# An attention and bilinear-FFN kernel whose instruction order is written by a planner: another transfer model in the planner, earlier start of the first pairs, and fewer dependencies on the first FFN products

## The chip, the cores and the metric

The kernel runs on one core of a Trainium2 chip. The metric is the device time of one execution in microseconds, here the median of three timed runs. Beside the timed runs there is one profiled execution, and everything that is read from a trace belongs to that one execution.

TensorE is called PE, its weight loads PEld, VectorE DVE, ScalarE ACT, GpSimd POOL and SyncE SP. Each engine runs its own list of instructions strictly in order, so an instruction that waits holds back all that stand behind it in the same list. SP and ACT also issue the transfers (DMAs); an issue row stands under SPq or ACTq.

## The reference

Inputs are q, k, v of shape (8, 12, 448, 64), two gains of 64 numbers, and three FFN weights in double precision: `w_a` and `w_b` (768 x 1536) and `w_out` (1536 x 768).

```python
q_n = q / sqrt(mean(q*q, -1) + 1e-6) * g_q          # the same for k with g_k
scores = q_n @ k_n.T / sqrt(64)
attn = softmax(scores)                              # over the keys
x = (attn @ v)  -> rows of (batch*seq, heads*64) = (3584, 768)
out = ((x @ w_a) * (x @ w_b)) @ w_out               # (3584, 768), float32
```

## The kernel before, in words

**Pairs of heads.** The 96 heads are worked off as 48 pairs, p = 0 to 47, six pairs to a batch row. For a pair, SP loads q, k and v (224 KB each, two buffers of each kind). `normalize(p)` squares q and k on ACT (`sq`, L435), sums the squares on DVE (`ms`, L442), takes the mean (L449), raises it to the power -0.5 on POOL (L453), and multiplies q by it on DVE (`qn`, L457). The k side is not multiplied: its factor goes into the exponential as a scale. `transposes(p)` turns k and qn on PE (`pt`, L486); ACT copies both to `qkT` (L491, L493). `scores` are four chunks of keys per pair on PE (`sc`, L506), each followed by two exponentials on ACT (`ET`, L512). `values` multiplies them with v (`o`, L527). For the first twelve pairs the sums over the keys are made on PE with a matrix of ones (`su`, L562); later pairs add on DVE and POOL first.

On PE a pair p makes two chains that are not interrupted: chain A holds the scores of chunks 0 and 1 of pair p and the values and sums of chunks 2 and 3 of pair p-1; chain B holds the scores of chunks 2 and 3 of pair p and the values and sums of its chunks 0 and 1. The transposes of the next pair stand between chains.

**The division.** The key sums of a pair are copied out of PSUM by ACT (`rec`, L581), spread over partitions by a transfer (`few`, L587), inverted on DVE (L598), written to DRAM (`inv`, L591) and read back to all partitions (L595). Then DVE multiplies the outputs with them (`x`, L624). I call these three transfers the round trip of the reciprocals.

**Weights.** `factors(n)` makes one of 18 sets of weights (12 of `w_a` and `w_b`, n = 0 to 11, and 6 of `w_out`, n = 12 to 17) from doubles: two loads of 768 KB issued by ACT, one ACT step (L268), six DVE steps (L269 to L277) and four DVE additions (L377), and a store of the finished set (`kept`, 1344 KB) issued by ACT. The words land in room that later tiles use: `hraw` in the tile of `hT` for the "early" sets, `lraw` in the tile `late` for the others. There are three `st` buffers for finished sets. The FFN works on two batch rows at once (four times, beta = 0 to 3), each matrix product made of seven products of half size (`pq`, L779, then `po`, L707); T2, T3 and T4 are differences of the four quarters of x, made by DVE in `combine` (L643).

**What sets the order.** No engine list is written by hand. Every piece of work is entered with `op(engine, us, key, emit, reads, writes, ...)`, and `Plan.run` (L70) is a list scheduler: it keeps a clock per engine, takes the engine whose next piece can start first, and among the pieces that can start about then the one with the lowest key. Its costs are the numbers `us`; a transfer of `kb` kilobytes is costed on a line of its own per issuing engine (L143 to L147). The planned times are used for the order alone; on the chip each instruction waits for what it depends on. `GATES` and `seq` (L877) say behind which pair's scores each weight set may be loaded and in which order; `WARM` says how many groups of four 128x128 matmuls (`warm`, L868) are put on PE with the lowest urgency.

Of the kernel before, what the change touches and what calls it, by code (L numbers as in the profile page):

```python
# [9 lines left out]
FP32 = mybir.dt.float32  # L10
# [15 lines left out]
class Plan:  # L26
# [10 lines left out]
    LANES = 8  # L37
    LAG = 0.1
# [31 lines left out]
    def run(self):  # L70
# [18 lines left out]
        opened, free, modes, cands, dma, port = {}, {}, {}, {}, {"SP": 0.0, "ACT": 0.0}, 0.0  # L89
# [21 lines left out]
        while any(cands.values()):  # L111
# [56 lines left out]
def kernel(  # L168
# [127 lines left out]
    def fast_body(ld, wk, ps_s, ps_o, ps_mm, dram):  # L296
# [4 lines left out]
        WARM = 12  # L301
# [40 lines left out]
        def factors(n, key, early, after):  # L342
# [16 lines left out]
            for part in range(2):  # L359
# [9 lines left out]
                op("ACT", 0.45, key - 2.5, load, after, [f"{row}/{part}"], kb=768)  # L369
# [38 lines left out]
        def loads(p, nm):  # L408
# [12 lines left out]
            op("SP", 0.5 if nm != "k" else 0.9, p - (1.8 if nm == "v" else 2.0), emit, [], [t], new=[t], kb=230)  # L421

        def normalize(p):

            ms, key = tile_of(f"ms{p}", "ms", 3), p - NORM
            for s, nm in enumerate("qk"):
                sq = tile_of(f"sq{nm}{p}", "sq", 1)

                def square(nm=nm):
# [4 lines left out]
                    if p < LEAD or SQUARE == "ACT":  # L434
                        nc.scalar.activation(t, flat, AF.Square)  # L435
                    else:
                        two[SQUARE].tensor_tensor(t, flat, flat, ALU.mult)

                def reduce(nm=nm, s=s):
                    if s == 0:  # L440
                        rs[p] = wk.tile([SP, 2, 2 * NJ], FP32, tag="ms", name="ms", bufs=3)
                    nc.vector.tensor_reduce(rs[p][:, s], xs["sq", nm, p], AX, ALU.add)  # L442
                e = "ACT" if p < LEAD else SQUARE
                op(e, {"ACT": 0.65, "POOL": 1.05, "DVE": 0.7}[e], key, square, [f"{nm}{p}"], [sq], new=[sq], lock=e != "ACT")
                op("DVE", 0.69, key, reduce, [sq], [ms], new=[ms] if s == 0 else [])

            def mean():
                msf = rs[p].rearrange("p s n -> p (s n)")
                nc.vector.tensor_scalar(msf, msf, 1.0 / D, 1e-6, ALU.mult, ALU.add)  # L449

            def root():
                msf = rs[p].rearrange("p s n -> p (s n)")
                nc.gpsimd.tensor_tensor(msf, msf, expo, ALU.pow)  # L453
# [8 lines left out]
            op("DVE", 0.18, key, mean, [], [ms])  # L462
            op("POOL", 2.95, key, root, [], [ms])
            qn = tile_of(f"qn{p}", "qn", 1)
            op("DVE", 0.7, key, apply, [ms, f"q{p}"], [qn], new=[qn], lock=True)
# [33 lines left out]
        def scores(p, c, chain):  # L499
# [16 lines left out]
            op("ACT", 1.12, p, exps, [sc, f"ms{p}"], [E], new=[E])  # L516
# [30 lines left out]

        def sums_over_keys(p, cs, chain):
# [19 lines left out]
            if p % (2 * HP) == 2 * HP - 1:  # L568
# [28 lines left out]
            op("SP", 0.8, p - 3.0, spread_out, [t], [few], new=[few], kb=20, dmas=2)  # L597
            op("DVE", 0.25, p - 3.0, lambda: nc.vector.reciprocal(fews[0], fews[0]), [], [few])  # L598
            op("SP", 0.4, p - 3.0, leave, [few], [f"inv{p}"], kb=20)
            op("SP", 0.8, p - 3.0, come_back, [f"inv{p}"], [t], kb=230, dmas=2)  # L600
# [8 lines left out]
        def put_out(p):  # L609
# [16 lines left out]
            op("DVE", 0.65, p, divide, [f"su{p}" if p % (2 * HP) == 2 * HP - 1 else f"rec{p}"], [f"{x}/{c}"], lock=True)  # L626
# [136 lines left out]
        def quarter_products(beta, key, m, ab, st, at, names, h):  # L763
# [6 lines left out]
            def product(bank, f, x, start, stop):  # L770
# [11 lines left out]
                op("PE", KH * S / 595, key, emit, [f"{st}/{(0, 0, 0, 0, 4, 5, 6)[f]}", *parts(x), *parts(T3), *parts(T4)], [nm, "ffn"], new=[nm] if start else [], mode="full")  # L782
# [94 lines left out]
        GATES = [0, 0, 1, 2, 3, 5, 7, 9, 10] + [12] * 9  # L877
        seq = [12, 13, 14, 15, 16, 0, 1, 2, 3, 4, 5, 6, 7, 17, 8, 9, 10, 11]
        for p in range(NP + 1):
            for x, n in enumerate(seq):  # L880
                if p == GATES[x]:
                    factors(n, x * 1.1 + 0.5, x < 8, [f"scored{p - 1}"] if p else [])
            if p < NP:
                for nm in "qkv":
                    loads(p, nm)
            if p == 0:
# [166 lines left out]
```

## Time and profile before

| what | value |
|---|---|
| median of three timed runs | 1647.89 us (1640.82 to 1650.4) |
| profiled execution, its own time | 1654.08 us |
| its span (first to last instruction) | 1652.2 us |
| mean granted PE clock | 0.989 of full |
| PE busy | 1604.7 us, 97% of the span |
| DVE / ACT / POOL busy | 729.3 / 432.7 / 401.8 us |
| moved by transfers | 191.21 MB |

PE's busy time includes matmuls that run at a lower clock; a matmul group of the same form at two durations tells of it. The idle time of an engine is listed with what ended it. Start times in a timeline are microseconds from the span's start. The profiled execution lies 6.2 us above the median of the timed runs.

### The profile page before, as it was taken

What the parts mean: (1) busy time and instruction counts of PE and PEld (TensorE: products, weight loads), DVE (VectorE), ACT (ScalarE), POOL (GpSimd) and SP (SyncE); (2) the same over time, 40 slices, a digit from 0 to 9 for tenths busy, and PEclk for the clock granted to TensorE, in tenths of its full rate; (3) what the DMA queues carried; (4) which work ended last, traced back from release to release, by engine and by line L of the source; (5) the groups of instructions that cost most, each with busy time, mean ns of one, the idle gap of its engine ahead of it and who ended that gap; (6) DMA issues with size and microseconds to landing.
All of it is one profiled execution on the core that took longest, in us unless ns stands there. A gap on an engine that the chain in (4) does not pass through costs nothing.

```text
span 1652.2 us, 15068 instructions
## 1 busy us (share of the span) xinstructions
PE 1604.7 (97%) x5546; PEld 786.7 (48%) x5546; DVE 729.3 (44%) x992; ACT 432.7 (26%) x777; POOL 401.8 (24%) x200
## 2 busy tenths in 40 slices
PE   7888799999999999999999999999999999999998
PEld 5333344455444455555444455555544555555554
DVE  4776657789567532222267541122235422222331
ACT  4666563311355610000255620000034000000000
POOL 3232354211366620100265630000133000100000
PEclk9999999999999999999999999999999999999999
DMA  5676325354433443212232333322222332222121
GB/s 183 229 228 219 122 68 183 100 209 149 147 97 99 117 141 123 100 67 100 80 97 85 107 104 129 109 71 96 96 68 81 110 134 100 96 71 91 70 103 50
DMA packets 131656, 191.21 MB, mean 116 GB/s; under 512 B 62196, under 2 KB 120308, under 8 KB 121844
## 3 DMA queue, kind: packets, MB, share of 16 engines
q1 hardware_dynamic: 103828, 137.06, 25.8%
q10 hardware_dynamic: 27744, 53.09, 8.9%
q8 instruction: 46, 0.75, 0.2%
q14 instruction: 38, 0.31, 0.1%
HBM read 154.01 MB, written 35.94 MB: 115 GB/s over the span
## 4 chain that ended last, share of the span: by engine, by line
PE 83%; DMA 7%; DVE 6%; issue 1%; ACT 1%; POOL 1%; SPq 1%; ACTq 0%; DVEq 0%; POOLq 0%
PE pq L779 43%; PE po L707 23%; PE sc L506 6%; PE o L527 6%; DMA inv<-few 2%; PE su L562 2%; DMA few<-rec 2%; PE pt L486 2%; DMA rec<-inv 1%; DVE x L643 1%; DMA k_sb<-in_k_dram 1%; DVE st L377 1%; POOL ms L453 1%; DVE st L277 1%; DVE su L572 1%
## 5 line engine op out<-in xcount | busy, mean ns | idle before, releaser
L779 PE MATMUL pq<-x,st 128*128 128x448 f32 x2016 | 768.3, 542 | 3.2 <-DVE t L836 3.2
L779 PEld LDWEIGHTS pq<-x,st 128*128 128x128 f32 x2016 | 381.9, 191 | 378.7 <-issue 368.3
L512 ACT ACTIVATE ET<-sc,ms 112x448 f32<-112x448 f32 x384 | 216.2, 637 | 128.4 <-PE sc L506 117.5
L707 PE MATMUL po<-st,hT 128*128 128x384 f32 x744 | 247.3, 488 | 0.0
L542 POOL TENSOR_TENSOR sum<-sum,ET 112x896 f32<-112x896 f32 x72 | 162.2, 2253 | 197.9 <-DVE sum L540 180.1
L453 POOL TENSOR_TENSOR ms<-ms,expo 112x16 f32<-112x16 f32 x48 | 152.6, 3180 | 214.7 <-DVE ms L449 203.5
L506 PE MATMUL sc<-qkT 64*112 64x448 f32 x768 | 175.1, 573 | 26.2 <-ACT ET L512 14.1
L827 POOL TENSOR_TENSOR hT<-hT,t 128x448 f32<-128x448 f32 x24 | 27.9, 1164 | 676.4 <-DVE t L825 676.4
L707 PEld LDWEIGHTS po<-st,hT 128*128 128x128 f32 x744 | 139.4, 190 | 102.2 <-issue 9.5
L527 PE MATMUL o<-ET,v_sb 112*64 112x448 f32 x768 | 168.1, 560 | 1.0 <-ACT x L620 1.0
L707 PE MATMUL po<-st,fin 128*128 128x384 f32 x432 | 145.1, 489 | 0.0
L801 ACT COPY hT<-pq 128x448 f32<-128x448 f32 x24 | 12.8, 532 | 447.0 <-PE pq L779 447.0
L506 PEld LDWEIGHTS sc<-qkT 64*112 64x112 f32 x768 | 61.2, 175 | 120.0 <-issue 79.0
L707 PEld LDWEIGHTS po<-st,fin 128*128 128x128 f32 x432 | 80.6, 190 | 59.3 <-issue 7.0
L527 PEld LDWEIGHTS o<-ET,v_sb 112*64 112x64 f32 x768 | 51.1, 140 | 106.9 <-issue 101.5
L442 DVE TENSOR_REDUCE ms<-sq 112x8 f32<-112x512 f32 x96 | 65.1, 678 | 73.5 <-ACT sq L435 69.7
L727 DVE TENSOR_TENSOR o_sb<-fin,po 128x384 f32<-128x384 f32 x56 | 31.0, 554 | 149.9 <-PE po L707 146.2
L457 DVE TENSOR_TENSOR qn<-q_sb,ms 112x512 f32<-112x512 f32 x48 | 62.6, 1304 | 22.2 <-POOL ms L453 11.2
L839 POOL TENSOR_TENSOR hT<-hT,t 128x448 f32<-128x448 f32 x48 | 58.9, 1229 | 46.7 <-DVE t L836 46.7
L804 ACT COPY t<-pq 128x448 f32<-128x448 f32 x24 | 12.8, 533 | 187.2 <-PE pq L779 187.2
L832 DVE TENSOR_TENSOR hT<-U,pq 128x448 f32<-128x448 f32 x48 | 29.8, 621 | 68.2 <-PE pq L779 68.2
L836 DVE TENSOR_TENSOR t<-U,pq 128x448 f32<-128x448 f32 x48 | 29.6, 620 | 65.0 <-PE pq L779 63.9
(70 smaller groups left out, 980.8 us busy)
## 6 DMA issues: line engine op xcount, KB each, us to landing
st<-kept SPq DMA_DIRECT2D x36, 1344.0 KB
st<-kept_o SPq DMA_DIRECT2D x28, 1152.0 KB
kept<-st ACTq DMA_DIRECT2D x12, 1344.0 KB
q_sb<-in_q_dram SPq DMA_DIRECT2D x48, 224.0 KB
k_sb<-in_k_dram SPq DMA_DIRECT2D x48, 224.0 KB
v_sb<-in_v_dram SPq DMA_DIRECT2D x48, 224.0 KB
rec<-inv SPq DMA_DIRECT2D x88, 112.0 KB
kept_o<-st ACTq DMA_DIRECT2D x6, 1344.0 KB
```

What stands on the lines that cost most here:

```text
L442: nc.vector.tensor_reduce(rs[p][:, s], xs["sq", nm, p], AX, ALU.add)
L453: nc.gpsimd.tensor_tensor(msf, msf, expo, ALU.pow)
L457: nc.vector.tensor_tensor(qns[p].rearrange("p j h d -> p h j d"), xs["q", p].rearrange("p h (j d) -> p h j d", d=D), rs[p][:, 0].rearrange ...
L486: nc.tensor.transpose(t[:, j * SP:(j + 1) * SP], x[:, j].rearrange("p h d -> p (h d)"), ident[0:SP, 0:SP])
L506: nc.tensor.matmul(t[:, e, 0:S], lhsT=qkTs[p][rows, 1, c * SP:(c + 1) * SP], rhs=qkTs[p][rows, 0, :], start=True, stop=True)
L512: nc.scalar.activation(E[:, e], scs[p, c][:, e, 0:S], AF.Exp, scale=rs[p][:, 1, 2 * c + e:2 * c + e + 1])
L527: nc.tensor.matmul(os_[p][e * D:(e + 1) * D, :], lhsT=xs["v", p][:, e, c * D:(c + 1) * D], rhs=ETs[p, c][:, e], start=(c == 0), stop=(c == ...
L542: two[ADD_UP].tensor_tensor(sums[p], sums[p], ETs[p, c], ALU.add)
L562: nc.tensor.matmul(sus[p][e * D:(e + 1) * D, :], lhsT=ones, rhs=x[:, e], start=(first and n == 0), stop=(last and n == len(parts) - 1))
L707: nc.tensor.matmul(held["po"][:, 0:HALF], lhsT=a[0]()[:, c], rhs=sts[beta, 12 + place_of[f]][:, c], start=(c == 0), stop=(c == MH - 1))
L779: nc.tensor.matmul(banks[bank][:, 0:S], lhsT=sts[at][:, f, c * P:(c + 1) * P], rhs=quads[x][:, c], start=(start and c == 0), stop=(stop an ...
L839: lambda i=i, n=n, nm=nm: two[TIMES].tensor_tensor(C(i, n), C(i, n), held[nm], ALU.mult), [t], [hp[i]],
```

## The change

Five things are changed in the tables and rules from which the order is made; the arithmetic stays, but for one instruction that is split.

1. The planner costs all transfers on one common line, `RATE` 300 KB per us and `LANDING` 2.5 us, in place of a line each for SP and ACT. Loads get a key 0.5 lower, and the round trip of the reciprocals a key 3 higher (less urgent).
2. For pairs 0 to 3 (`APART`) the mean and the power run for q and for k apart, as two POOL instructions of 112x8 in place of one of 112x16, and the scale of the exponentials depends on k's alone.
3. `WARM` goes from 12 to 4 (16 warm matmuls in place of 48).
4. `GATES` and `seq` are other numbers, five sets are early in place of eight, and the loads of the first weight sets wait for the k of pair 0.
5. The seven half-size products of the FFN no longer name T3 and T4 among what they read, only what they use.

```diff
-        opened, free, modes, cands, dma, port = {}, {}, {}, {}, {"SP": 0.0, "ACT": 0.0}, 0.0
+        opened, free, modes, cands, dma, port = {}, {}, {}, {}, 0.0, 0.0
...
-                    dma[e] = max(dma[e], t) + ops[x][7] / (200.0 if dma["SP" if e == "ACT" else "ACT"] > t else 250.0)
-                    end[x] = dma[e] + 2.5
+                    dma = max(dma, t) + ops[x][7] / self.RATE
+                    end[x] = dma + self.LANDING
                     sent += [end[x]] * ops[x][11]
-                    if e == "SP":
-                        dma["ACT"] = max(dma["ACT"], t) + ops[x][7] / 300.0
...
-        WARM = 12
+        WARM = 4
+        APART = 4
...
-                op("ACT", 0.45, key - 2.5, load, after, [f"{row}/{part}"], kb=768)
+                op("ACT", 0.45, key - 1.5, load, after, [f"{row}/{part}"], kb=768)
...
-            op("SP", 0.5 if nm != "k" else 0.9, p - (1.8 if nm == "v" else 2.0), emit, [], [t], new=[t], kb=230)
+            op("SP", 0.5 if nm != "k" else 0.9, p - (2.3 if nm == "v" else 2.5), emit, [], [t], new=[t], kb=230 if nm != "k" else 400)
...
+            def roots(a, b, names):
+                msf = lambda: rs[p][:, a:b].rearrange("p s n -> p (s n)")
+                op("DVE", 0.18, key, lambda: nc.vector.tensor_scalar(msf(), msf(), 1.0 / D, 1e-6, ALU.mult, ALU.add), [], names)
+                op("POOL", 1.7 if b - a == 1 else 2.95, key,
+                   lambda: nc.gpsimd.tensor_tensor(msf(), msf(), expo[:, 0:2 * NJ * (b - a)], ALU.pow), [], names)
...
+            sums(0, "q")
+            if p < APART:
+                roots(0, 1, [f"{ms}/q"])
+            sums(1, "k")
+            if p < APART:
+                roots(1, 2, [f"{ms}/k"])
+            else:
+                roots(0, 2, [f"{ms}/q", f"{ms}/k"])
...
-            op("SP", 0.8, p - 3.0, spread_out, [t], [few], new=[few], kb=20, dmas=2)
+            op("SP", 0.8, p - 0.0, spread_out, [t], [few], new=[few], kb=20, dmas=2)
...
-                op("PE", KH * S / 595, key, emit, [f"{st}/{(0, 0, 0, 0, 4, 5, 6)[f]}", *parts(x), *parts(T3), *parts(T4)], [nm, "ffn"], new=[nm] if start else [], mode="full")
+                op("PE", KH * S / 595, key, emit, [f"{st}/{(0, 0, 0, 0, 4, 5, 6)[f]}", *parts(x)], [nm, "ffn"], new=[nm] if start else [], mode="full")
...
-        GATES = [0, 0, 1, 2, 3, 5, 7, 9, 10] + [12] * 9
-        seq = [12, 13, 14, 15, 16, 0, 1, 2, 3, 4, 5, 6, 7, 17, 8, 9, 10, 11]
+        GATES = [0, 0, 1, 1, 1, 2, 2, 2, 2, 2, 3, 5, 6, 6, 8, 8, 9, 10]
+        seq = [13, 12, 16, 14, 15, 0, 1, 2, 3, 4, 5, 6, 7, 8, 9, 10, 17, 11]
...
-                    factors(n, x * 1.1 + 0.5, x < 8, [f"scored{p - 1}"] if p else [])
+                    factors(n, x * 1.1 + 1.5, x < 5, [f"scored{p - 1}"] if p else ["k0"])
```

Since the order comes from the planner, the diff does not show which instruction stands where. Three places follow; a trailing xN counts equal instructions in a row, and line numbers are those of each kernel.

The first place is ACT's list from its start. `hraw` is the landing room of the weight words, `sq` the squares, `gain` a small constant, `qkT` the turned q and k, `ET` the exponentials. Before:

```order
L231 ACT_TABLE_LOAD
L231 ACTIVATE grow<-const-float32-0.0 1x256
L364 DMA hraw<-in_moe_w_out_dram 128x1536 x4
L435 ACTIVATE sq<-q_sb 112x512
L435 ACTIVATE sq<-k_sb 112x512
L863 COPY gain<-pg 128x1
L491 COPY qkT<-pt 128x448
L435 ACTIVATE sq<-q_sb 112x512
L493 ACTIVATE qkT<-pt,gain 128x448
L268 ACTIVATE st<-hraw 128x1536
L435 ACTIVATE sq<-k_sb 112x512
L512 ACTIVATE ET<-sc,ms 112x448 x6
```

And in the changed kernel:

```order
L440 ACTIVATE sq<-q_sb 112x512
L440 ACTIVATE sq<-k_sb 112x512
L364 DMA hraw<-in_moe_w_out_dram 128x1536 x2
L867 COPY gain<-pg 128x1
L364 DMA hraw<-in_moe_w_out_dram 128x1536
L440 ACTIVATE sq<-q_sb 112x512
L364 DMA hraw<-in_moe_w_out_dram 128x1536
L492 COPY qkT<-pt 128x448
L440 ACTIVATE sq<-k_sb 112x512
L494 ACTIVATE qkT<-pt,gain 128x448
L513 ACTIVATE ET<-sc,ms 112x448 x4
```

The four issues of weight loads stood ahead of the first squares and now stand behind them, and the first rounding step (`st<-hraw`) no longer stands ahead of the first exponentials.

The second place is PE's list from its start; `warm` are the warm matmuls and `pg` a product that spreads the gains. Before:

```order
L868 MATMUL warm<-ident 128x128 x28
L860 MATMUL pg<-ones,grow 128x1
L868 MATMUL warm<-ident 128x128 x20
L486 MATMUL pt<-ident,k_sb 128x112 x4
L486 MATMUL pt<-ident,qn 128x112 x4
L506 MATMUL sc<-qkT 112x448 x8
L527 MATMUL o<-ET,v_sb 64x448 x4
L562 MATMUL su<-ET,ones 64x448 x4
```

And in the changed kernel:

```order
L872 MATMUL warm<-ident 128x128 x16
L864 MATMUL pg<-ones,grow 128x1
L487 MATMUL pt<-ident,k_sb 128x112 x4
L487 MATMUL pt<-ident,qn 128x112 x4
L507 MATMUL sc<-qkT 112x448 x4
L487 MATMUL pt<-ident,k_sb 128x112 x4
L487 MATMUL pt<-ident,qn 128x112 x4
L507 MATMUL sc<-qkT 112x448 x4
L528 MATMUL o<-ET,v_sb 64x448 x4
L566 MATMUL su<-ET,ones 64x448 x4
```

The second group of warm matmuls is gone, and the transposes of pair 1 stand between the two halves of pair 0's scores.

The third place is PE's list behind the transposes of the twelfth pair (p = 11), where the changed kernel has its first FFN product `pq`; before, it stood two pairs later.

```order
L487 MATMUL pt<-ident,qn 128x112 x4
L507 MATMUL sc<-qkT 112x448 x4
L528 MATMUL o<-ET,v_sb 64x448 x4
L566 MATMUL su<-ET,ones 64x448 x4
L507 MATMUL sc<-qkT 112x448 x4
L528 MATMUL o<-ET,v_sb 64x448 x4
L566 MATMUL su<-ET,ones 64x448 x4
L783 MATMUL pq<-x,st 128x448 x3
L507 MATMUL sc<-qkT 112x448 x4
```

That one product of three matmuls moved ahead of the thirteenth pair; the others keep their places between the chains of pairs 13 and later. From there on PE's list is the same but for the places of a few `po` products.

Where the DVE steps of the weight sets (ten to a set) stand, counted ahead of the n-th `qn` in DVE's list:

| n-th `qn` | 4 | 5 | 7 | 8 | 10 | 12 | 14 |
|---|---|---|---|---|---|---|---|
| weight steps ahead of it, before | 12 | 22 | 41 | 45 | 60 | 69 | 80 |
| weight steps ahead of it, changed | 3 | 13 | 25 | 33 | 48 | 64 | 80 |

More of the change, by code (lines that the diff above doesn't have):

```diff
@@ L37 @@
     LANES = 8
+    RATE, LANDING = 300.0, 2.5
     LAG = 0.1
@@ L433, in square @@
                             x.rearrange("p j h d -> p (j h) d"))
[L434 to L453, printed above, removed]
+                    nc.scalar.activation(t, flat, AF.Square)
+                op("ACT", 0.65, key, square, [f"{nm}{p}"], [sq], new=[sq])
+                op("DVE", 0.69, key, lambda: nc.vector.tensor_reduce(rs[p][:, s], xs["sq", nm, p], AX, ALU.add), [sq], [f"{ms}/{nm}"])
+            def roots(a, b, names):
[3 more added lines that the diff above has]
+                   lambda: nc.gpsimd.tensor_tensor(msf(), msf(), expo[:, 0:2 * NJ * (b - a)], ALU.pow), [], names)
             def apply():
@@ L461, in apply @@
                     ALU.mult)
-            op("DVE", 0.18, key, mean, [], [ms])
-            op("POOL", 2.95, key, root, [], [ms])
+            sums(0, "q")
[6 more added lines that the diff above has]
+                roots(0, 2, [f"{ms}/q", f"{ms}/k"])
             qn = tile_of(f"qn{p}", "qn", 1)
-            op("DVE", 0.7, key, apply, [ms, f"q{p}"], [qn], new=[qn], lock=True)
+            op("DVE", 0.7, key, apply, [f"{ms}/q", f"q{p}"], [qn], new=[qn], lock=True)
         def transposes(p):
@@ L515, in scores @@
                mode="rows", chain=chain)
-            op("ACT", 1.12, p, exps, [sc, f"ms{p}"], [E], new=[E])
+            op("ACT", 1.12, p, exps, [sc, f"ms{p}/k"], [E], new=[E])
         def values(p, c, chain):
```

23 lines of the change are left out of this document (14 added, 9 removed).

## The prediction

> **What bounds the kernel now.** I began with the busy time of the engines and with PE's waits over the whole span.
>
> ```profile
> PE 1604.7 (97%) x5546; PEld 786.7 (48%) x5546; DVE 729.3 (44%) x992; ACT 432.7 (26%) x777; POOL 401.8 (24%) x200
> PE sc L506 <- ACT ET L512: 14.1, 8, 3.5
> PE sc L506 <- ACT qkT L493: 12.0, 5, 5.2
> PE pq L779 <- DVE t L836: 3.2, 2, 1.9
> ```
>
> PE is the bound, and its waits are short: the columns are total, count and longest. They are not spread evenly, so next I took the busy times by stretches; the columns are start and end, length, then busy time of PE, PEld, DVE, ACT and POOL with the instructions, the granted clock, the transfers' busy share and their rate.
>
> ```profile
> 0.00:21.75 21.75, 16.93 (x106) 16.55 (x107) 3.39 (x9) 4.76 (x9) 3.76 (x9) 0.84 0.64 221
> 150.00:212.00 62.00, 49.39 (x214) 18.58 (x212) 38.77 (x50) 32.44 (x60) 21.74 (x8) 0.89 0.50 155
> 212.00:318.00 106.00, 102.98 (x382) 45.10 (x378) 69.08 (x88) 48.59 (x83) 43.98 (x20) 1.00 0.41 132
> 318.00:435.00 117.00, 116.80 (x306) 58.69 (x306) 98.02 (x110) 16.52 (x19) 16.17 (x11) 0.99 0.45 169
> 633.00:1652.20 1019.20, 1010.22 (x3172) 514.14 (x3170) 318.24 (x467) 154.55 (x291) 180.61 (x102) 1.00 0.28 93
> ```
>
> From 212 us on PE is idle for a few microseconds in 106 and for 9 in 1019, at full clock. The change leaves PE's list there all but untouched, so nothing is to be won or lost behind 212 us but through lateness. The question is how much of the first 212 us, start and twelve pairs, it takes away.
>
> **The start.** These rows of the timeline lead from the first landings to the first exponential (start, length, instruction; in brackets the idle time before and what ended it).
>
> ```profile
> 5.86 0.60 SPq L416 DMA_DIRECT2D k_sb<-in_k_dram  x1
> 8.93 0.82 ACTq L364 DMA_DIRECT2D hraw<-in_moe_w_out_dram  x2
> 9.80 0.63 ACT L435 ACTIVATE sq<-q_sb 112x512 f32<-112x512 f32 x1 [7.35 <-DMA k_sb<-in_k_dram]
> 10.46 0.69 DVE L442 TENSOR_REDUCE ms<-sq 112x8 f32<-112x512 f32 x1 [10.46 <-ACT sq L435]
> 12.56 0.17 DVE L449 TENSOR_SCALAR ms<-ms 112x16 f32<-112x16 f32 x1
> 12.89 2.92 POOL L453 TENSOR_TENSOR ms<-ms,expo 112x16 f32<-112x16 f32 x1 [11.44 <-DVE ms L449]
> 15.85 0.69 DVE L457 TENSOR_TENSOR qn<-q_sb,ms 112x512 f32<-112x512 f32 x1 [3.11 <-POOL ms L453]
> 12.03 7.66 PE L868 MATMUL warm<-ident 128*128 128x128 f32 x40
> 19.91 0.55 PE L486 MATMUL pt<-ident,qn 112*128 112x112 f32 x4
> 21.75 1.76 PE L506 MATMUL sc<-qkT 64*112 64x448 f32 x8 [1.29 <-ACT qkT L493]
> 23.59 1.68 ACT L512 ACTIVATE ET<-sc,ms 112x448 f32<-112x448 f32 x3
> ```
>
> Three delays are to be seen. The square of q waits behind two weight-load issues of ACT that go out at 8.93, when the first k has landed, though SP's next issue went out at 5.86 and q was then there. The power waits for q and k together and takes 2.92 us. And qn is ready at 16.54 (15.85 + 0.69), but the transposes start only when 40 rows of warm matmuls end, at 19.5.
>
> In the changed order all three go. I work with landings at 5.9 for q and 8.9 for k, as now; they are upper bounds, since the two weight loads of 768 KB that ran beside them now wait for k. Square of q to 6.5, sum to 7.2, mean to 7.4. The power on 112x8 is in no row: it lies between 1.46 (half of 2.92, if it goes by elements) and 2.92 (if it does not). I take 2.2, the middle. So POOL ends at 9.6, qn at 10.3, its transposes with 0.55 at 10.9, the copy by ACT at about 11.5, and the first scores follow at 11.7. On k's side: square to 9.5, sum to 10.2, mean to 10.4, power to 12.6, first exponential at 12.7 in place of 23.59: 10.9 us earlier, 10.2 with the dearer power and 12 with the cheaper one and k landed at 7.2. The load of v and the gains run beside it.
>
> Pair 1 now needs its powers from the same POOL: with 2.2 each they end at 14.8 for its q and 17.0 for its k. Its qn is then done at 15.5, its transposes at 16, the second half of pair 0's scores at 18, and the values and sums of that pair's first half (3.2 us) at 21.2. So pair 1's first scores start at about 21.2, where they now start at 33.75 (row below): **12.5 us earlier**, 11 to 14 by the same bounds. What is gained beyond 10.9 is that no rounding step stands ahead of the exponentials any more.
>
> The warm matmuls that went are priced by what a cold PE costs here.
>
> ```profile
> 66.95 3.33 PE L506 MATMUL sc<-qkT 64*112 64x448 f32 x8 [3.50 <-ACT ET L512]
> 70.21 2.99 PE L527 MATMUL o<-ET,v_sb 112*64 112x448 f32 x8
> 33.75 1.76 PE L506 MATMUL sc<-qkT 64*112 64x448 f32 x8 [2.82 <-ACT qkT L493]
> 35.44 1.72 PE L527 MATMUL o<-ET,v_sb 112*64 112x448 f32 x8
> 179.51 3.33 PE L506 MATMUL sc<-qkT 64*112 64x448 f32 x8 [5.24 <-ACT qkT L493]
> ```
>
> After a wait of 3.5 us the same two groups took 6.3 in place of 3.5 us, so being cold costs 2.8 us once. With PE idle from about 5 to 10.9 us the first groups will be cold. There, though, the exponentials are later than PE: two for each chunk at some 0.56 us against a group of scores of 1.76 for two chunks, so I charge nothing for it; without that cover it is 2.8. The Trainium skill, in "TensorE: Matmul & The Clock Gate", section "What's actually happening", gives the reason: the array's clock is halved until it has been busy for about 3.4 us, and again after as long an idle window. By that rule the change throws away a paid warm-up, and the sum would come out some 3 us higher; the rows agree with it in size.
>
> **The twelve pairs.** From 33.75 to 179.51 PE does eleven pairs, 145.8 us or 13.25 each. An undisturbed chain with transposes takes 5.76 us (33.75 to the scores at 39.51) and one without 4.85 (124.50 to 129.35):
>
> ```profile
> 39.51 1.76 PE L506 MATMUL sc<-qkT 64*112 64x448 f32 x8
> 124.50 1.76 PE L506 MATMUL sc<-qkT 64*112 64x448 f32 x8
> 129.35 0.60 PE L486 MATMUL pt<-ident,k_sb 112*128 112x112 f32 x4
> ```
>
> That is 10.6 a pair and 116.7 for eleven: 29 us are waits and the cold clock that follows them. Their causes stand in the waits of ACT and DVE and in one example.
>
> ```profile
> 54.28 0.67 SPq L416 DMA_DIRECT2D k_sb<-in_k_dram  x1
> 65.22 0.63 ACT L435 ACTIVATE sq<-k_sb 112x512 f32<-112x512 f32 x1 [5.36 <-DMA k_sb<-in_k_dram]
> ACT sq L435 <- DMA k_sb<-in_k_dram: 15.8, 3, 7.3
> DVE few L598 <- DMA few<-rec: 20.4, 5, 6.8
> DVE x L624 <- DMA rec<-inv: 8.8, 3, 4.4
> ```
>
> A load of 224 KB issued at 54.28 lands at 65.2, eleven microseconds later; ACT stands before its square for 5.36 us with the exponentials behind it, PE runs dry (the 3.50 at 66.95) and comes back cold. The same happens on DVE before a late reciprocal, with the next qn behind it. So the stalls come from transfers that are slower than the planner thought, when weights move beside them. The new planner counts ACT's and SP's transfers on one line, and a small load behind two weight loads is costed as late as it is; but at 300 KB per us plus 2.5 it would still land well before those eleven.
>
> What I can count is the load. Ahead of the seventh qn DVE now has 25 weight steps in place of 41, ahead of the fourteenth 80 as before. A step is 1.03 us on the mean: eight sets took 82.0 us in 80 steps, by the sum of the groups of which two rows are shown.
>
> ```profile
> L377 DVE TENSOR_TENSOR st<-st 128x384 f32<-128x384 f32 x32 | 17.1, 555 | 0.6
> L272 DVE SCALAR_TENSOR_TENSOR st<-hraw,st 128x1536 uint32<-128x1536 uint32 x8 | 14.0, 1755 | 0.1
> ```
>
> Adding up my excess over the nominal steps, 14 us of the 29 lie before the scores at 98.96 and 15 behind them. In the first half 16 steps less (16.5 us of DVE) and fewer weight transfers stand in the way, and I take two thirds of the 14 off: 9 us. In the second half as many steps come on top, with a planner that sees transfers better: I take no gain. The bounds are 26 (nearly all waits go) and -3.5 (9 won early, and 12 steps more between the eighth and the fourteenth qn, 47 for 35, all surface on PE: 12.5).
>
> **The other edits.** The loads' lower keys bring no load ahead of its free buffer, so they cost and give nothing beyond the pace above. The first product ahead of the thirteenth pair needs the sixth weight set; 64 steps stand ahead of the qn that precedes it, so it does not wait, and it only moves 2.4 us of work into a place where PE might otherwise idle: nothing. Products without T3 and T4 wait for less; in the old list only a handful stand where that matters. Four more POOL instructions are hidden, as POOL is idle most of the early stretch.
>
> **Sum.** 12.5 + 9 = 21.5 us less. The profiled execution's 1654.1 would become 1632.6; it lies 6.2 above the median of the timed runs, so the median goes from 1647.9 to **1626**. The likeliest case's own range is 1614 to 1637.
>
> **The rivals.**
>
> *The waits all but vanish.* If the planner's new line puts each square and reciprocal behind its landing, 26 of the 29 go: 12.5 + 26 gives 1609. For it: all long waits have this one cause. Against it: the line is costed at 300 KB per us, and the transfers moved 221 KB per us or less in these stretches.
>
> *The weights crowd the later pairs.* The 12.5 us of extra DVE steps between the eighth and the fourteenth qn appear on PE: 12.5 + 9 - 12.5 leaves 9, or 1639. For it: 47 steps and six pairs' own normalizing (2.2 us each by the rows of the start) are 62 us on DVE in six pairs that PE would do in 64, with the division still to come. Against it: DVE's longest idle times there are waits for transfers, which steps can fill.
>
> *The change does not carry to the end.*
>
> ```profile
> L779 PE MATMUL pq<-x,st 128*128 128x448 f32 x2016 | 768.3, 542 | 3.2 <-DVE t L836 3.2
> L836 DVE TENSOR_TENSOR t<-U,pq 128x448 f32<-128x448 f32 x48 | 29.6, 620 | 65.0 <-PE pq L779 63.9
> ```
>
> PE reaches the long run of products earlier, and those need weight sets: DVE is busy for 98.02 of 117 us there. PE spends 16.0 us on the 42 rows of a set (768.3 over 2016 each), DVE ten steps and five or six additions of 0.62, some 13.7, so it holds pace; but if the buffers hand back the whole pace gain and half the start, 6 us are left: 1642.
>
> *Slower: the round trip of the reciprocals, now ranked last, is late where it is needed.*
>
> ```profile
> 133.60 6.42 DMA few<-rec
> 149.63 3.21 DMA inv<-few
> 153.45 8.05 DMA rec<-inv
> ```
>
> One such trip is 17.7 us in transfers alone. Before the FFN the divided outputs of pairs 9 to 11 must go through the subtractions that form T2, and DVE has two of these reciprocals close together in the changed list. If DVE stands before a whole trip twice, with qn behind it, PE waits for 35 us and comes back cold twice (5.6): 41 - 21.5 gives 19 more, 1667. It decides from 22 us of such waits on; one trip alone gives 1647. For it: a wait of 6.8 us on this very transfer exists. Against it: between trip and use lies more than a pair, and the longest wait for the read-back was 4.4.
>
> **Chances.** Forecast 0.54; waits vanish 0.15; crowding 0.16; not carried 0.08; slower 0.07. A measurement of this kernel tells a change of about 0.5%, 8.2 us, from none: 1639.7 to 1656.1 counts as the same. Faster: 0.54 + 0.15 + 0.6 of the crowding, 0.10, less a little for the forecast's tail, 0.78. The same: 0.14. Slower: 0.08. For eight in ten the range reaches to the vanished waits and to the case that is not carried: 1608 to 1643.
>
> **What would show it.** Right: the first `ET` at 11 to 13 us, pair 1's first scores at 20 to 23, the pq run that now starts at 318 us some 20 us earlier, and the same spacing behind it. Pair 1 behind 27 would break the start; a spacing of 13.2 us a pair between it and the thirteenth pair would break the second term, with ACT's `sq` or DVE's `few` still waiting for transfers. PE idle in the pq run would speak for the third rival, a long DVE wait before `few` or `x` near the thirteenth pair for the last.

## The result, and the profile after

The changed kernel takes 1604.17 us (median of four, 1600.51 to 1606.7), against 1647.54 before: a ratio of 0.9741, with a 95% interval of 0.9704 to 0.9777. It is faster, as forecast, but by 43 us where 21.5 were worked out, and below the range of 1608 to 1643. Its profiled execution spans 1603.9 us (1652.2 before), so 48.3 are to be accounted for there; some 5 of them belong to the two profiled executions alone, which lie 6.2 us (before) and 1.5 us (changed) above the medians.

From the page of the changed kernel come the busy times, the chain that ended last, and the largest group (its last number is the idle time of PE before it).

```profile
PE 1584.2 (99%) x5482; PEld 776.6 (48%) x5482; DVE 718.9 (45%) x996; ACT 434.0 (27%) x777; POOL 403.2 (25%) x204
...
PE 88%; DVE 1%; issue 0%; ACT 0%; DVEq 0%
...
L783 PE MATMUL pq<-x,st 128*128 128x448 f32 x2016 | 764.3, 540 | 0.0
```

Before, PE was busy for 1604.7 us: 20 us of the gain is work that takes less time. Thirty-two warm matmuls are gone, and fewer groups run cold. The rest, 28 us, is idle time of PE (span less busy time: 47.5 us before, 19.7 now). Transfers, 7% of the chain before, no longer appear in it. Here are PE's waits of the changed kernel over the whole span (total, count, longest).

```profile
PE sc L507 <- ACT qkT L494: 8.6, 5, 3.0
PE warm L872 <- POOL expo L232: 1.4, 1, 1.4
PE su L566 <- DVE x L628: 1.2, 1, 1.2
PE sc L507 <- ACT ET L513: 0.6, 2, 0.4
```

The 14.1 us of waits for exponentials have become 0.6. The waits for `t` in the product runs (3.2 us) are gone.

Where the 48.3 us came from shows in the first scores of some pairs and the long runs of products behind them; the times are starts of rows in PE's timeline.

| | before | changed | won so far |
|---|---|---|---|
| pair 1, first scores | 33.75 | 20.71 | 13.0 |
| pair 7 | 111.51 | 85.00 | 26.5 |
| pair 12 | 179.51 | 147.80 | 31.7 |
| first long run of products (before, a piece at 302.49 and the one at 318.20), start | 302.49 | 260.69 | 41.8 |
| its end | 435.10 | 389.42 | 45.7 |
| span | 1652.2 | 1603.9 | 48.3 |

Of the changed kernel's windows (columns as in the prediction), these carry it; the last is the product run.

```profile
20.70:147.80 127.10, 121.97 (x624) 47.00 (x622) 109.61 (x149) 94.15 (x165) 48.15 (x14) 0.99 0.77 246
34.00:180.00 146.00, 139.32 (x701) 53.94 (x698) 124.01 (x168) 103.05 (x184) 59.24 (x18) 0.99 0.72 229
260.70:389.40 128.70, 128.70 (x344) 65.03 (x342) 105.58 (x126) 21.80 (x26) 24.13 (x15) 1.00 0.47 171
```

And of the kernel before, the second of these stretches:

```profile
34.00:180.00 146.00, 125.11 (x618) 46.85 (x618) 102.52 (x142) 90.41 (x160) 41.90 (x12) 0.95 0.68 218
```

In the same 146 us PE does 701 rows of matmuls in place of 618 (the trace has two rows for a matmul of the instruction list), and DVE, which also has its work to do there, is busy for 124 in place of 102.5 us. The transfers do not move much more: 229 GB/s for 218. What has gone is standing before them. These are the waits of ACT and DVE for transfers between 20 and 212 us, of the changed kernel

```profile
DVE x L628 <- DMA rec<-inv: 2.7, 2, 2.3
ACT sq L440 <- DMA q_sb<-in_q_dram: 2.2, 2, 1.1
DVE few L602 <- DMA few<-rec: 1.4, 1, 1.4
ACT sq L440 <- DMA k_sb<-in_k_dram: 0.9, 1, 0.9
```

and, but for one row of 1.1, of the one before:

```profile
DVE few L598 <- DMA few<-rec: 20.4, 5, 6.8
DVE x L624 <- DMA rec<-inv: 8.8, 3, 4.4
ACT sq L435 <- DMA k_sb<-in_k_dram: 8.4, 2, 5.4
ACT sq L435 <- DMA q_sb<-in_q_dram: 6.3, 2, 4.9
ACT ET L512 <- DMA few<-rec: 4.7, 1, 4.7
ACT ET L512 <- DMA kept_o<-st: 4.5, 1, 4.5
```

7.2 us are left of 54.2 (the sums of all such rows of ACT and DVE). I call this sum the transfer waits below; it comes from one profiled execution of each kernel.

**The start** came out at the forecast times. Its rows in the changed kernel:

```profile
5.20 3.87 POOL L448 TENSOR_TENSOR ms<-ms,expo 112x8 f32<-112x8 f32 x2 [3.75 <-DVE ms L446]
5.31 0.63 ACT L440 ACTIVATE sq<-k_sb 112x512 f32<-112x512 f32 x1 [1.19 <-DMA k_sb<-in_k_dram]
6.88 0.69 DVE L452 TENSOR_TENSOR qn<-q_sb,ms 112x512 f32<-112x512 f32 x1
8.08 0.55 PE L487 MATMUL pt<-ident,qn 112*128 112x112 f32 x4
8.22 1.77 ACTq L364 DMA_DIRECT2D hraw<-in_moe_w_out_dram  x1
10.03 0.53 ACT L492 COPY qkT<-pt 128x448 f32<-128x448 f32 x1 [1.20 <-issue]
11.67 2.21 PE L507 MATMUL sc<-qkT 64*112 64x448 f32 x8 [3.04 <-ACT qkT L494]
12.79 2.30 ACT L513 ACTIVATE ET<-sc,ms 112x448 f32<-112x448 f32 x4 [1.17 <-PE sc L507]
20.71 1.76 PE L507 MATMUL sc<-qkT 64*112 64x448 f32 x8
```

First scores at 11.67 (forecast 11.7), first exponential at 12.79 (12.7), pair 1 at 20.71 (21.2). The way there differs: the squares of q and k start at 3.5 and 5.3 where I had the landings at 5.9 and 8.9, and qn is done at 7.6 where I had 10.3; but then ACT's list stands at a weight-load issue for 1.77 us (8.22 to 9.99) ahead of the copy that the scores need. Two squares of pair 1 (0.63 each) also stand in ACT's list before the copies are done. The errors cancel, and the first exponential, which I had waiting for the power of k, waits 1.17 us for the scores.

The first groups are cold, 2.21 in place of 1.76, and that is paid for. PE waits for nothing between 11.67 and 20.71, and the granted clock falls to half on the way; `u_gk`, one of the experiments below, runs the same groups in the same order at full clock. First a stretch of the changed kernel, then two rows of `u_gk`:

```profile
13.80:15.50 1.70, 1.70 (x10) 1.41 (x9) 0.00 (x0) 1.70 (x4) 0.34 (x1) 0.50 1.06 377
10.60 1.76 PE L507 MATMUL sc<-qkT 64*112 64x448 f32 x8 [2.20 <-ACT qkT L494]
18.08 1.76 PE L507 MATMUL sc<-qkT 64*112 64x448 f32 x8
```

From pair 0 to pair 1 it is 9.04 us in the changed kernel and 7.48 in `u_gk`: the cold clock costs 1.6 us.

### The profile page after: what moved, and what is told of

The parts are those of the page before. It is cut to its first block, busy times and chain, and to the rows that moved or that the text cites. A ratio compares the mean times of both kernels' runs of the same rounds, so it can differ in the third digit from the quotient of the medians.

```text
span 1603.9 us, 14949 instructions
## 1 busy us (share of the span) xinstructions
PE 1584.2 (99%) x5482; PEld 776.6 (48%) x5482; DVE 718.9 (45%) x996; ACT 434.0 (27%) x777; POOL 403.2 (25%) x204
## 4 chain that ended last, share of the span: by engine, by line
PE 88%; DVE 1%; issue 0%; ACT 0%; DVEq 0%
PE pq L783 47%; PE po L711 24%; PE sc L507 7%; PE o L528 7%; PE su L566 2%; PE pt L487 2%; DVE x L647 1%; DVE su L576 0%; DVE x L628 0%; DVE qn L452 0%; DVE ms L442 0%; DVE o_sb L731 0%; ACT sq L440 0%; DVE ms L446 0%; DVE sum L541 0%
## 5 line engine op out<-in xcount | busy, mean ns | idle before, releaser
L448 POOL TENSOR_TENSOR ms<-ms,expo 112x16 f32<-112x16 f32 (+1 forms) x52 | 159.1, 3060 | 189.0 <-DVE ms L446 182.1
L507 PE MATMUL sc<-qkT 64*112 64x448 f32 x768 | 171.8, 565 | 9.3 <-ACT qkT L494 8.6
L528 PE MATMUL o<-ET,v_sb 112*64 112x448 f32 x768 | 164.0, 548 | 0.0
```

The source lines that it names most:

```text
L448: lambda: nc.gpsimd.tensor_tensor(msf(), msf(), expo[:, 0:2 * NJ * (b - a)], ALU.pow), [], names)
L507: nc.tensor.matmul(t[:, e, 0:S], lhsT=qkTs[p][rows, 1, c * SP:(c + 1) * SP], rhs=qkTs[p][rows, 0, :], start=True, stop=True)
L528: nc.tensor.matmul(os_[p][e * D:(e + 1) * D, :], lhsT=xs["v", p][:, e, c * D:(c + 1) * D], rhs=ETs[p, c][:, e], start=(c == 0), stop=(c == ...
```

## The experiments

The question was which of two readings is true. The first puts the gain down to the common line: it makes the planner see transfers late where they are late. The rival puts it down to the other edits: the gates and the early weights, or the first products that are no longer held. Sixteen kernels were run. Any edit makes the planner write a new order, so a single edit undone also changes places that it has nothing to do with; that is why the same question was asked from several sides.

### One part undone in the changed kernel

The first two belong together, since with the old line there is no order unless T3 and T4 are named again. `u_t34` names them (the last pair of lines); `u_line_t34` also has the old line.

```diff
-                    dma = max(dma, t) + ops[x][7] / self.RATE
-                    end[x] = dma + self.LANDING
+                    dma[e] = max(dma[e], t) + ops[x][7] / (200.0 if dma["SP" if e == "ACT" else "ACT"] > t else 250.0)
+                    end[x] = dma[e] + 2.5
...
+                    if e == "SP":
+                        dma["ACT"] = max(dma["ACT"], t) + ops[x][7] / 300.0
...
-    [f"{st}/{(0, 0, 0, 0, 4, 5, 6)[f]}", *parts(x)]
+    [f"{st}/{(0, 0, 0, 0, 4, 5, 6)[f]}", *parts(x), *parts(T3), *parts(T4)]
```

> The changed kernel with the old transfer lines in the planner (one each for SP and ACT) and with T3 and T4 named again (without them this order cannot be planned); compare it with the run that only names T3 and T4 again. Theory A (the common line makes the order that waits for nothing): pairs 1 to 12 go back to some 13 us each, 15 to 20 us lost, 1620 to 1626 us. Theory B (the gates did it, by moving weight steps out of the first pairs): at most 5 us lost, under 1611.

> The changed kernel with T3 and T4 named again among what each product reads. Only the first product should go back behind the thirteenth pair. Both theories: the spacing of the pairs stays at 11.5 us and the time within 4 us of the changed kernel, 1602 to 1608. If holding the first product costs more than its own 2.4 us, 1610 or more.

Measured: 1616.06 with T3 and T4 named (0.9812, interval 0.9792 to 0.9833), and 1667.98 with the old line as well (1.0138, 1.0114 to 1.0162). The line is worth 52 us between these two orders, and without it the other edits make the kernel 22 us slower than it was before. The start is not to blame: pair 1 of `u_line_t34` comes at 21.35. Its window and two of its transfer waits:

```profile
34.00:180.00 146.00, 114.82 (x556) 43.23 (x552) 97.49 (x131) 81.89 (x143) 32.76 (x10) 0.88 0.64 202
```

```profile
DVE few L604 <- DMA few<-rec: 10.9, 4, 5.0
ACT ET L515 <- DMA v_sb<-in_v_dram: 7.8, 1, 7.8
```

PE does 556 rows where it did 701, at a clock of 0.88, and the transfer waits are back at 38 us. Planned with the old line, the same edits keep the early start and lose it again before pair 12 (182.25, against 179.51 before the change).

`u_t34` loses 12 us although its transfer waits stay at 9.4. In its PE timeline:

```profile
144.66 2.94 PE L507 MATMUL sc<-qkT 64*112 64x448 f32 x8 [3.78 <-ACT qkT L494]
...
165.79 3.35 PE L783 MATMUL pq<-x,st 128*128 128x448 f32 x4 [2.52 <-DVE x L647]
```

Pair 12 comes earlier than in the changed kernel (144.66 for 147.80, where 2.45 are the moved product); the loss lies behind it, in a wait for the turned q and at the first products, which wait for DVE's subtractions.

Four more undo one part each:

```diff
u_gk:    GATES and seq as before; five early sets and the wait for k of pair 0 stay
u_rec:   -  op("SP", 0.8, p - 0.0, spread_out     +  op("SP", 0.8, p - 3.0, spread_out   (and the three behind it)
u_apart: -  APART = 4                             +  APART = 0
u_warm:  -  WARM = 4                              +  WARM = 12
```

> The changed kernel with the old GATES and seq numbers, all else as changed. Theory A: the planner still sees the transfers rightly and works around the earlier weights: 1604 to 1610. Theory B: weight steps come back into the first pairs and with them the waits: 1614 to 1625.

> The changed kernel with the round trip of the reciprocals ranked as before (key p - 3 in place of p). Theory A: same, 1602 to 1608. Theory C (its low rank lets the loads of q and k go first on SP and ends the late landings): waits of ACT for q and k come back, 1612 to 1622.

> The changed kernel with q and k of the first four pairs normalized together again. By the working of the start, the power of pair 0 ends at 13.3 in place of 9.6 for q (both squares, both sums, then 2.9 us): first scores at 15.4 in place of 11.7, 3 to 4 us lost, 1607 to 1609; nothing lost if pair 1 is bound by something else.

> The changed kernel with the 48 warm matmuls back. If the warm-up is worth its place: pair 0 runs warm, up to 2.8 us won, 1601. If the warm matmuls stand in front of the first transposes as before: 5 to 8 us lost, 1609 to 1612.

Measured: 1605.79 (0.9753, 0.9733 to 0.9772), 1610.28 (0.9786, 0.9766 to 0.9806), 1606.54 (0.9748, 0.9724 to 0.9771) and 1617.35 (0.9818, 0.9794 to 0.9843). The gates and the splitting of the powers are worth next to nothing in the end. `u_gk` does not bring the load on DVE back, though, as one of its expectations had it: 25 weight steps stand ahead of its seventh `qn`, as in the changed kernel, so it tests the numbers in the tables and not the load. Splitting does what it says at the start: `u_apart` has pair 1 at 23.27, 2.6 us later, and has made up 1.6 of it by pair 12. `u_rec` lies between its two expectations, 6 us slower, with transfer waits of 14 us for 7; `u_warm` is slower than either of its own.

The warm matmuls lose twice. The rows of `u_warm` on PE:

```profile
12.18 1.96 PE L872 MATMUL warm<-ident 128*128 128x128 f32 x16
14.08 1.76 PE L507 MATMUL sc<-qkT 64*112 64x448 f32 x8
...
166.53 1.02 PE L783 MATMUL pq<-x,st 128*128 128x448 f32 x2 [2.27 <-DVE x L647]
170.30 5.59 PE L783 MATMUL pq<-x,st 128*128 128x448 f32 x8 [2.75 <-DVE x L647]
```

They stand in front of the first scores, which run at 1.76 in place of 2.21 but start 2.4 us later (14.08 for 11.67); being warm gives back 0.7 of that by pair 1 (22.44 for 20.71). Most of the 13 us are lost at pair 13, before the subtractions again, and that is a matter of the new order, not of warm matmuls. How much of the 13 they cost with everything else in its place was not isolated.

### One part done alone in the kernel before

```diff
b_line:   the common line alone
-         dma[e] = max(dma[e], t) + ops[x][7] / (200.0 if dma["SP" if e == "ACT" else "ACT"] > t else 250.0)
-         end[x] = dma[e] + 2.5
+         dma = max(dma, t) + ops[x][7] / 300.0
+         end[x] = dma + 2.5
b_gates:  GATES, seq, five early sets, loads of the first sets behind k of pair 0, keys of weight loads -1.5
-                    factors(n, x * 1.1 + 0.5, x < 8, [f"scored{p - 1}"] if p else [])
+                    factors(n, x * 1.1 + 1.5, x < 5, [f"scored{p - 1}"] if p else ["k0"])
```

> The kernel before with one edit alone, the common transfer line in the planner (300 KB per us, 2.5 us). Theory A (the line alone ends the waits of the pairs): the start stays at 33.75 us for the scores of pair 1, the pairs go at 11.5 to 12 us each, and 15 to 25 us are won: 1621 to 1632. Theory D (the line works only together with the later weights and the new keys): within 8 us of before, 1638 to 1654.

> The kernel before with the new GATES, seq, the five early sets and the wait of the first weight loads for the first k, but the old transfer lines, keys and warm matmuls. Theory A: the first squares no longer wait behind weight loads (some 3 us won), the pairs wait as before or more: 1642 to 1660. Theory B: the pairs speed up, 1625 to 1637.

Measured: the line alone 1626.81 (0.9875, 0.9848 to 0.9901), the gates and weights alone 1646.58 (0.9993, 0.9977 to 1.0008). The reading by the line holds, and the rival falls as far as the gates and weights go. The count of weight steps falls with it: ahead of the seventh `qn` stand 43 in `b_line`, more than the 41 before, and 26 in `b_gates`. The waits of `b_line`:

```profile
DVE x L622 <- DMA rec<-inv: 10.9, 5, 3.7
DVE few L596 <- DMA few<-rec: 7.9, 3, 3.0
ACT sq L433 <- DMA q_sb<-in_q_dram: 6.5, 3, 2.8
```

Its transfer waits are 29.9 us, between 54.2 and 7.2, and so is its time. This sum does not give the time by itself: in `b_gates` it is 34, hardly more, and nothing is won. What ACT and DVE wait for costs only what PE is kept waiting: PE is idle for 28.6 us of the span in `b_line`, for 42.2 in `b_gates`.

The rest of the way, from 1627 to 1604, comes with the other edits on top of the line: 10.1 us at the start (pair 1 at 30.81 for 20.71), 6.8 on the way to pair 12 (131.5 for 127.1, of which 2.45 are the moved product), the rest up to the products. No single undoing moves the time by that much, and two edits were undone in no run: the earlier keys of the loads, and a k that the planner costs at 400 KB in place of 230 (it stands in the diff, not in the list of five). What each gives on top of the line is open.

### Are the transfers really what is waited for?

`b_small` keeps the order of the kernel before, instruction for instruction, and loads only a sixth of the words of 13 of the 18 weight sets, so its products work on other weights; that is all that it leaves out.

```diff
-                            nc.scalar.dma_start(to, moe_w_out[k * P:(k + 1) * P, :])
+                            nc.scalar.dma_start(to[:, 0:256], moe_w_out[k * P:(k + 1) * P, 0:256])
```

> The kernel before, order untouched, but from the fourth early and the third late weight set on only a sixth of the words is loaded (13 of 18 sets; the weights and the output are then not the reference's). Theory E (PE's waits come from transfers that weights slow down): small loads land sooner, pairs 4 to 12 go at 11.5 us, 10 to 20 us won, 1627 to 1637. Theory F (the order itself makes the waits, by engines standing before one another): within 5 us of before.

Measured: 1633.65 (0.9917, 0.9895 to 0.9940). Its window and its longest waits:

```profile
34.00:180.00 146.00, 133.78 (x673) 50.80 (x670) 113.85 (x153) 99.28 (x177) 46.14 (x14) 0.96 0.58 181
```

```profile
DVE few L609 <- DMA few<-rec: 10.9, 4, 6.8
DVE x L635 <- DMA rec<-inv: 5.7, 5, 2.8
ACT sq L446 <- DMA k_sb<-in_k_dram: 4.8, 2, 2.7
```

With not one instruction moved, lighter weight traffic takes 14 us off the kernel and 22 off the transfer waits. So weights do hold the small transfers up. It is a third of the gain: an order that puts the consumers later gets more than lighter traffic does, with all the traffic there.

### Is it that the line is common, or its rate?

The kernel before, with other lines: two lines of 150 KB per us that do not know of each other; a common one at 1000, 400 and 600; and a common one at 300 with 5 us of landing.

```diff
b_two150:  +  dma[e] = max(dma[e], t) + ops[x][7] / 150.0     (no push of ACT's line by SP)
b_c1000:   +  dma = max(dma, t) + ops[x][7] / 1000.0          (b_c400: 400.0, b_c600: 600.0)
b_l5:      +  dma = max(dma, t) + ops[x][7] / 300.0;  end[x] = dma + 5.0
```

> The kernel before, planner with two lines as before but each at 150 KB per us and without the push of SP's transfers on ACT's. Theory G (what matters is that the planned total rate is near the chip's): like the common line alone, 1620 to 1632. Theory H (what matters is that SP's small loads stand behind ACT's weights on one line): no better than before, 1640 or more.

> The kernel before with the common line in the planner but at 1000 KB per us, so that hardly anything queues on it. Theories G and H: the planned landings are too early and the waits come back: 1640 or more. If it is as fast as the line at 300 (1620 to 1632), the size of the planned lateness does not matter and the gain is the luck of one order.

> The kernel before with the common line at 300 KB per us and 5 us in place of 2.5 for landing, so that every load is planned still later. Theory H: at least as few late landings as with 2.5, 1615 to 1630. If too much caution costs: planned pieces are held back, 1635 or more.

> The kernel before with the common line at 400 KB per us (300 gave 1627, 1000 gave 1651). Planned lateness as the cause: in between, nearer to 300: 1628 to 1640. Luck of single orders: anywhere from 1615 to 1660.

> The kernel before with the common line at 600 KB per us. Planned lateness: between the run at 400 and the one at 1000, 1638 to 1650. Luck: anywhere, for instance below the run at 400.

| line in the kernel before | us | ratio, interval | transfer waits, us |
|---|---|---|---|
| two at 150 | 1654.13 | 1.0039, 1.0024 to 1.0055 | 49 |
| common, 1000 | 1650.99 | 1.0018, 1.0003 to 1.0034 | 50 |
| common, 600 | 1641.03 | 0.9968, 0.9954 to 0.9983 | 44 |
| common, 400 | 1648.16 | 1.0007, 0.9993 to 1.0021 | 50 |
| common, 300 (`b_line`) | 1626.81 | 0.9875, 0.9848 to 0.9901 | 30 |
| common, 300, landing 5.0 | 1617.15 | 0.9812, 0.9791 to 0.9833 | 8 |

By these orders neither half is enough: not the total rate (two lines at 150 make 300), and not a common line (400 and up give nothing or next to nothing). It takes both. I had expected 1628 to 1640 at 400; it gave nothing. The step from 400 to 300 is also the step in the waits; `b_c400` still has

```profile
DVE few L596 <- DMA few<-rec: 19.0, 8, 4.2
ACT sq L433 <- DMA q_sb<-in_q_dram: 12.8, 4, 4.1
```

Within the two groups there is no steady trend: 600 is 7 us faster than 400. If more landing time helps the kernel before by another 10 us, it should help the changed one too, or do nothing there; that was the last pair of runs.

```diff
a_l45:    -  RATE, LANDING = 300.0, 2.5    +  RATE, LANDING = 300.0, 4.5
a_t_l50:  -  RATE, LANDING = 300.0, 2.5    +  RATE, LANDING = 300.0, 5.0    (and T3, T4 named)
```

> The changed kernel with 4.5 us in place of 2.5 for landing. Planned lateness: PE's losses of 9 us behind the start shrink to 3 to 6, 1597 to 1604. Luck: 1604 to 1620.

> The changed kernel with T3 and T4 named again (1616 so) and 5 us in place of 2.5 for landing. Planned lateness: faster than without, 1603 to 1613. Luck: either side of 1616.

Measured: 1620.72 (0.9852, 0.9834 to 0.9870) and 1619.03 (0.9839, 0.9822 to 0.9855). It hurts: `a_l45` is slower than either of its expectations, and `a_t_l50` than the 1616 that it was to beat. The transfer waits of `a_l45` are 6.1 for the 7.2 of the changed kernel, so there was next to nothing left to win by landing time; and the new order has other waits, such as this one on PE:

```profile
92.23 0.98 PE L487 MATMUL pt<-ident,qn 112*128 112x112 f32 x4 [6.96 <-DVE qn L452]
```

Taken together, all ten orders that were planned with a common line at 300 take 1604 to 1627 us, and all seven that were planned otherwise (the kernel before among them) 1641 to 1668. PE's idle time parts them in the same way, 20 to 30 us and 42 to 62. Between the groups the line decides. Within a group some 10 us to either side depend on what a re-planned order happens to do with qn, the turned q and the subtractions; the changed kernel is the best of its group, with `u_gk` and `u_apart` within 2.4 us of it.

## Why the prediction was right, and where it was wrong

**Right: what bounds the kernel.** 41.8 of the 48.3 us were won ahead of the long product run, by waits that are gone and the cold clock behind them, and what PE won at the pairs reached the end. The third rival (not carried) is out: the long product run of the table starts 41.8 us earlier and is shorter by 3.9, with PE busy in all of its 128.70 us.

**Right: the first term**, 13.0 for 12.5, with the bounds 11 to 14, and with some luck on the way to it. The power on 112x8, which I took at 2.2 between 1.46 and 2.92, has the mean 1.93 in the changed kernel's groups on POOL:

```profile
L448 POOL TENSOR_TENSOR ms<-ms,expo 112x8 f32<-112x8 f32 x8 | 15.4, 1928 | 17.0 <-DVE ms L446 16.9
```

The landings and what holds ACT up, both told above, cancel. Charging nothing for the cold PE was wrong: PE has no wait behind which the exponentials could hide it, and it cost 1.6 us of the 2.8 that I had put without cover. The rule of the Trainium skill ("TensorE: Matmul & The Clock Gate", "What's actually happening") fits in kind, with 2.21 for 1.76 in the first scores, though PE's idle time ahead of them is 3.04 us and not the 3.4 of the rule; of its 3 us about half are found.

**Wrong: the second term.** The first term holds, so the miss of the sum lies in what follows pair 1: 9 us by the forecast, 35 by the two profiles. I took 9 of the 29 us of excess. From pair 1 to pair 12 the kernel before takes 145.76 us, the changed one 127.09, and 2.45 of these are the first product that now stands there: 21.1 us won, 8 of excess left. 13.5 of them lie ahead of pair 7, 7.6 behind it, where I had taken "no gain". (The 14 us that the prediction counts before the scores at 98.96 are those ahead of pair 7, at 111.51; before 98.96 it is 12.)

The step that failed is the sentence on the planner: "but at 300 KB per us plus 2.5 it would still land well before those eleven". From it I concluded that the line changes little, and costed the load on DVE in its place. Both halves of this can be checked on the very transfer I used. Around it, before, SP and ACT issue:

```profile
52.38 1.18 SPq L595 DMA_DIRECT2D rec<-inv  x2
53.61 0.57 SPq L419 DMA_DIRECT2D v_sb<-in_v_dram  x1
54.13 0.53 ACTq L385 DMA_DIRECT2D kept_o<-st  x1
54.28 0.67 SPq L416 DMA_DIRECT2D k_sb<-in_k_dram  x1
```

By hand, from the issue times on the chip and with nothing queued before: by the old rule, with the planner's own sizes, three transfers of 230 at 200 KB per us from 52.38 on, plus 2.5, land at 58.3. By the common line the 1376 of `kept_o` stand in between: 2066 / 300 = 6.9, plus 2.5, lands at 61.8. (With the changed kernel's 400 for a k it would be 0.6 later.) The real landing was at 65.2. The new line is still too early, as I wrote, but it closes half of the gap, and it moves this transfer by 3.5 us against those that have no weights beside them. I compared the new cost with the truth and not with the old cost. And an order does not need the truth: it needs the consumers to come late enough, while other work fills the time, and DVE had that work (124 us busy for 102.5 in the same 146). The rival "the waits all but vanish", 1609 at a chance of 0.15, is what came by its mechanism; not by its sum, which took 26 of the 29 us where 21.1 came, and nothing behind pair 12. Its stated counter-argument, the 221 KB per us that the stretches moved, was no argument: the changed kernel moves 229 to 246 there and does not wait.

My other count, the 25 weight steps in place of 41 ahead of the seventh qn, stays true as a count, but the runs show that this load decides nothing: with 26 steps `b_gates` takes 1646.58, and with 43 and 46, more than before the change, `b_line` and `b_l5` take 1626.81 and 1617.15.

**Mis-sized: what follows pair 12.** I gave the first products "nothing". Between pair 12 and the product run another 7.6 us were won (122.98 for 112.89, less the 2.45 moved), 3.9 in the run and 2.6 behind it. `u_t34` puts the price of naming T3 and T4 at 12 us, lost in that place, though with another order around it. The rival of the crowded later pairs (12.5 us) did not come: PE waits for 5.4 us in all between 120 and 260 us.

**The slower rival** (a round trip in the way, 1667) did not come. That `u_line_t34` takes 1668 is a coincidence of numbers: the rival had DVE standing for 35 us before two round trips, and there it stands for 12.6 in all before `few` and `x`.

**Open.** What decides inside a group of orders is not settled: why 600 plans a better order than 400, and why one undone edit costs 2 us and another 13. One candidate is out: how far ahead of its square a k is issued. For pairs 1 to 12 the median is 8.5 us before the change, 9.5 after it and 9.3 in `u_gk`. What each edit adds on top of the line, among them the two that no run undid, is open too.

## What to carry to other kernels

Where an order is planned, a planner that costs transfers too early shows in the trace as short waits of many engines for small transfers; look for it there before moving any work, and compare the new cost with the old cost, not only with the truth. A shared resource wants one line with a margin: at 300 KB per us and 2.5 to 5 us of landing all ten orders were good, at 400 and above (with 2.5 us) none of three. Measure by the time and by PE's idle time; the waits of the other engines only point to the cause. When a change re-plans everything, undo and redo each part, hold the order fixed once (as `b_small` does), check in the new order that the undoing took back what it was meant to (`u_gk` did not), and believe a single undoing only beyond the spread of its group, here some 10 us.

## What the runs showed of the hardware

The rate that plans well lies below what the transfers reach in a burst. In the kernel before, 40 to 66 us, in 40 slices:

```profile
GB/s 173 92 192 378 400 402 399 402 397 444 407 416 400 408 380 172 2 0 0 0 0 138 178 170 337 403 402 398 354 290 260 391 413 429 381 446 391 383 176 22
```

Some 400 GB/s while weights move, and yet the 224 KB of k, issued at 54.28 with a 1344 KB transfer of ACT's ahead, and two weight loads issued by 57.6 behind it, took 10.9 us: 224 KB at 400 would be 0.6. The rate falls off at 65 us, where it landed: the small transfer came in with the large ones that another engine had issued around it, not ahead of them.

The power on POOL is not priced by its elements alone. On 112x8 it takes 1.93 us on the mean (1.64 at the least), on 112x16 of the same kernel, up to 100 us,

```profile
L448 POOL TENSOR_TENSOR ms<-ms,expo 112x16 f32<-112x16 f32 x6 | 26.0, 4330 | 38.2 <-DVE ms L446 38.2
```

4.33, where one at the start of the kernel before took 2.92: the same instruction half as long again in the busy stretch. Why was not tested.
